# A two-stage attention and channel-mix kernel on one core: deferred gate mixes, another key order, slab weight sums, squares on ScalarE, operand sums on VectorE, another product order

## Chip, core and metric

The kernel runs on one core of a Trainium2 chip. The metric is the device time of one launch in microseconds, here the median of three runs. The engines are named as in the profile: PE is TensorE (PEld is its loading of stationary operands), DVE is VectorE, ACT is ScalarE, POOL is GpSimd, and SP only issues DMAs, in its program order.

## What is computed

The reference is capped attention, whose output x is then mixed and put through a squared-ReLU network with a sigmoid gate. Cut to what matters:

```python
# q, k, v: (8, 12, 448, 64); x: (8, 448, 768)
s = cap * tanh((q @ k.T) / 8 / cap)
a = exp(s - max(s)); a = a / (sum(a) + 1e-9)
x = (a @ v) laid out as (batch, token, 768)
x_prev = x shifted by one token, zero first
xk = mu_k * x + (1 - mu_k) * x_prev
xr = mu_r * x + (1 - mu_r) * x_prev
k = relu(xk @ w_k)            # 768 -> 1024
v = (k * k) @ w_v             # 1024 -> 768
r = sigmoid(xr @ w_r)         # 768 -> 768
out = r * v
```

The three weight matrices come as 64-bit floats and are made into 32-bit floats on the chip. Large products are done as three products of rounded high and low parts (hi·hi, hi·lo, lo·hi).

## The kernel before

**Stage 1.** The 12 heads of a batch are 6 head pairs, so there are 48 pairs, and step i works on several pairs at once. The string `STEP` (L51 to L53) sets the order of operations in a step; each engine executes its own in that order. Scores, tanh, exp and row sums (`red`, L238) belong to pair i; the gather of row sums (`gather`, L243, four DMAs), their reciprocals (`recip`, L247 to L251: sr, rs) and the product with v to pair i-1; `norm` (L263, writes x), the key mix (`mix_old` on ACT, `mix_new` on DVE, tile xk), its high and low parts (POOL, tiles xkh and xkl) and the gate mix to pair i-2. The gate mix is `gate_old` on POOL (L292) and then `gate_new` on DVE (L295), in tile xg, which `x_store` (L299) writes to x_d in DRAM for stage 2. SP issues, in a step: gather (sq<-r), rv<-v, a weight load, rec_store, rqk<-qk, two r<-rec_d, x_d<-xg, and a store of a finished weight; then the next step's gather.

**Keys.** From step 7 on (`LAG`), PE also does the key matmuls of a batch whose six pairs are mixed: 144 of them per batch for 8 columns of blocks (fc), spread over six steps, four calls of six in each. `key_order` (L301) sets their order; a column block needs 18 matmuls (6 dc by 3 parts) into one of two PSUM banks (kps), which ACT empties as ko (L329) and stores to k_d.

**Weights.** 44 pieces of w_k, w_r and w_v are loaded, cleaned on DVE (L381 to L389) and summed on POOL (L396); pieces of w_k also go through POOL wkh (L74) and DVE wkl (L409). In steps 6 to 10 two pieces are loaded a step.

**Stage 2.** There are 28 units of 256 tokens: 14 value units (k·k times w_v) and then 14 gate units (xr times w_r, sigmoid, times v). Each is a 2 by 2 block product by the Strassen-Winograd scheme, with 7 products P1 to P7, one in each slot: 12 matmuls of 128x384 in a value unit's slot, 9 in a gate unit's. `ahead(g)` (L583) issues beside slot g the work of later slots: the loads (src, L481, ten slots ahead), squares (L486, eight ahead), the sums of operand blocks on POOL (`sums2`, L501 to L507, four ahead), and the high part on ACT (L521) and low part on DVE (L522) of the operand two slots ahead. `evacuate` (L540) takes products out of four PSUM banks: p1 is copied, u2 and u3 add it (L556), and the outputs add u2 or u3 (L560).

**Between them.** In the tail (steps 49 to 54) SP loads w_v from DRAM in 16 DMAs of one 128x384 block (L430, L435), and `w2_prep` makes the sums and the high and low parts of seven products' weights, block by block, on DVE (L446 to L466) and ACT (L445); the same is done for w_r during the value units, on DVE and ACT. The code of the prep and the sums is in two places of the program, of which one (for large caps) is not executed.

```python
            for _ in prep:
                pass
            self.k_store()
            self.w2_pool("r", pool("w2r", 1))
            self.w2_loads("r")
            for g in range(2 * NU * SLOTS + 3):
                self.slot(g)
```

Of the kernel before, what the change touches and what calls it, by code (L numbers as in the profile page):

```python
# [1 line left out]

# [7 lines left out]
F32 = mybir.dt.float32  # L10
# [33 lines left out]
P1, P2, P3, P4, P5, P6, P7 = range(7)  # L44

# [6 lines left out]
weight_sum tanh1 exp1 red1 norm recip rec_store K qk_high qk_low tanh2 mix_old mix_new x_high x_low gate_old relu k_store  # L52
K exp2 red2 weight_rest weight_sum relu k_store S3 K K tanh3 exp3 red3 gate_new relu k_store weight_abs load_qk rec_load x_store weight_store"""  # L53
# [6 lines left out]
class Body:  # L60
# [239 lines left out]

    def key_order(self):  # L301
# [120 lines left out]
    def w2_pool(self, kind, pool):  # L422
        n = (NF if kind == "v" else ND) // 2
        self.W2[kind] = tuple(pool.tile([P, 7, n, HN], F32R, name=f"w{kind}{x}") for x in "hl")

    def w2_load(self, kind, j):
        lo = self.W2[kind][1]
        n, at = lo.shape[2], (ND if kind == "v" else 0)
        for m, c, h in ((P1, j, 0), (P3, j + n, 1), (P2, j + n, 0)):
            self.nc.sync.dma_start(f(lo[:, m, j, :]), self.w_d[at + c, :, h * HN:(h + 1) * HN])  # L430

    def b12_load(self, kind, j):
        if j < self.W2[kind][1].shape[2]:
            t = self.b12[kind, j] = self.st.tile([P, HN], F32, name=("p1", "u2")[j % 2])
            self.nc.sync.dma_start(t, self.w_d[j + (ND if kind == "v" else 0), :, HN:])  # L435

    def w2_loads(self, kind):
        for j in range(self.W2[kind][1].shape[2]):
            self.w2_load(kind, j)
            if j < 2:  # L440
                self.b12_load(kind, j)

    def w2_split(self, kind, m, j, x):
        hi, lo = (w[:, m, j, :] for w in self.W2[kind])
# [353 lines left out]
```

## Time and profile before

| what | us |
|---|---|
| median of 3 runs | 1000.93 (1000.39 to 1002.9) |
| the profiled execution, its own time | 998.11 |
| its span, first to last instruction | 995.8 |
| PE busy in the span | 914.0 |
| DVE busy | 801.2 |
| ACT busy | 600.7 |
| POOL busy | 500.8 |

The span is the part of the profiled execution that the trace shows; 2.3 us lie around it. The mean clock granted to TensorE over the span is 0.969 of full speed. The median of the runs is 2.8 us above the profiled execution, so a time worked out on the trace is read on the trace's own scale first.

### The profile page before, as it was taken

To read this page: it belongs to the slowest core of one execution; us is meant where nothing else is said; L and a number is where in the kernel's file an instruction comes from. 1 tells how busy PE (TensorE), PEld (TensorE's weight loads), DVE (VectorE), ACT (ScalarE), POOL (GpSimd) and SP (SyncE) were. 2 spreads that over 40 slices of the span, in tenths; PEclk is the share of its full clock that TensorE was granted. 3 is DMA by queue.
4 is the path that set the end of the run, shared out by engine and by line. 5 is a ranking of instruction groups with operands and counts; after the bars stand their busy time and mean duration, and the time that the engine had idled before them with its cause. 6 is when DMAs were issued, how large, how long until landed. Compare 5 with 4: busy or idle time off the path is not lost.

```text
span 995.8 us, 15130 instructions
## 1 busy us (share of the span) xinstructions
PE 914.0 (92%) x4986; PEld 722.7 (73%) x4986; DVE 801.2 (80%) x1305; ACT 600.7 (60%) x887; POOL 500.8 (50%) x418
## 2 busy tenths in 40 slices
PE   7778779999999999999999777999999999999997
PEld 3235556667666766766676667989898999999996
DVE  7888999888888888887677575898888766887785
ACT  7766657787888887887877333334333334444543
POOL 4667766667666665776653222334342433333331
PEclk9788998999999999999999897999999999999999
DMA  5445544665665566565443535343433326666663
GB/s 157 142 137 166 192 140 163 200 202 186 214 215 175 205 205 206 184 194 185 146 138 99 198 119 175 98 140 97 134 107 117 123 92 203 204 194 208 204 207 115
DMA packets 118871, 163.95 MB, mean 165 GB/s; under 512 B 22400, under 2 KB 102912, under 8 KB 118784
## 3 DMA queue, kind: packets, MB, share of 16 engines
q1 hardware_dynamic: 109568, 148.21, 46.6%
q10 hardware_dynamic: 9216, 14.68, 3.9%
q8 instruction: 41, 0.67, 0.3%
q14 instruction: 46, 0.38, 0.1%
HBM read 106.70 MB, written 53.39 MB: 161 GB/s over the span
## 4 chain that ended last, share of the span: by engine, by line
PE 37%; DVE 22%; POOL 10%; DMA 10%; issue 9%; SPq 5%; ACT 5%; ACTq 0%; DVEq 0%; POOLq 0%
PE ps L537 25%; PE kps L322 6%; DMA sq<-r 4%; SPq L243 4%; PE s L194 3%; DVE r L238 3%; DVE lo L522 3%; POOL xg L292 3%; PE pv L221 3%; DMA src<-x_d 3%; POOL xkl L84 2%; DVE xg L295 2%; ACT p L212 2%; POOL qkl L84 2%; DVE o L560 1%
## 5 line engine op out<-in xcount | busy, mean ns | idle before, releaser
L238 DVE TRANSPOSE_TENSOR_REDUCE r<-p 128x28 f32<-128x896 f32 (+1 forms) x240 | 218.6, 919 | 48.1 <-ACT p L212 43.5
L202 ACT ACTIVATE p<-s,scl_t 128x896 f32<-128x896 f32 x192 | 173.6, 904 | 45.7 <-PE s L194 39.4
L212 ACT ACTIVATE p<-p,cap_t 128x896 f32<-128x896 f32 x192 | 182.0, 948 | 10.2 <-ACT ko L329 5.4
L322 PE MATMUL kps<-xkh,wkh 128*128 128x448 f32 x384 | 147.0, 383 | 16.2 <-ACT ko L329 15.3
L501 POOL TENSOR_TENSOR s<-src 128x512 f32<-128x512 f32 (+1 forms) x28 | 32.6, 1166 | 251.9 <-DVE src L486 154.9
L537 PE MATMUL ps<-wvh,hi 128*128 128x384 f32 x392 | 135.3, 345 | 22.2 <-DVE o L560 11.1
L322 PE MATMUL kps<-xkl,wkh 128*128 128x448 f32 x384 | 140.7, 366 | 0.6 <-POOL xkl L84 0.6
L322 PE MATMUL kps<-xkh,wkl 128*128 128x448 f32 x384 | 140.9, 367 | 0.0
L521 ACT CAST hi<-s 128x512 fp32r<-128x512 f32 (+1 forms) x112 | 63.5, 567 | 118.9 <-PE ps L537 87.0
L537 PE MATMUL ps<-wvl,hi 128*128 128x384 f32 x392 | 132.8, 339 | 0.0
L221 PE MATMUL pv<-p,rv 128*64 128x448 f32 x576 | 132.0, 598 | 0.0
L522 DVE TENSOR_TENSOR lo<-s,hi 128x512 fp32r<-128x512 f32 (+1 forms) x112 | 82.5, 737 | 48.9 <-ACT hi L521 32.1
L194 PE MATMUL s<-qkh 64*128 64x448 f32 (+1 forms) x336 | 85.1, 447 | 29.8 <-ACT p L202 24.9
L396 POOL TENSOR_TENSOR wsq<-wa,wsq 128x384 f32<-128x384 f32 x44 | 44.6, 1014 | 133.9 <-DVE wsq L389 133.9
L521 ACT CAST hi<-src 128x512 fp32r<-128x512 f32 (+1 forms) x84 | 47.7, 568 | 100.3 <-PE ps L537 83.3
L84 POOL TENSOR_TENSOR qkl<-rqk,qkh 128x960 fp32r<-128x960 f32 x47 | 106.2, 2259 | 3.9
L537 PE MATMUL ps<-wrh,hi 128*128 128x384 f32 x294 | 99.9, 340 | 6.2 <-DVE o L560 5.8
L194 PEld LDWEIGHTS s<-qkh 64*128 64x128 f32 (+1 forms) x336 | 37.3, 190 | 86.9 <-ACT p L202 34.9
L322 PEld LDWEIGHTS kps<-xkh,wkh 128*128 128x128 f32 x384 | 72.9, 190 | 37.8 <-ACT ko L329 18.5
L537 PE MATMUL ps<-wrl,hi 128*128 128x384 f32 x294 | 98.7, 336 | 0.0
L522 DVE TENSOR_TENSOR lo<-src,hi 128x512 fp32r<-128x512 f32 (+1 forms) x84 | 74.1, 882 | 28.4 <-PE ps L537 15.1
L537 PEld LDWEIGHTS ps<-wvh,hi 128*128 128x128 f32 x392 | 75.0, 191 | 28.3 <-ACT hi L521 14.7
(93 smaller groups left out, 1854.7 us busy)
## 6 DMA issues: line engine op xcount, KB each, us to landing
rqk<-qk SPq DMA_DIRECT2D x47, 480.0 KB
k_d<-ko ACTq DMA_DIRECT2D x64, 224.0 KB
src<-k_d SPq DMA_DIRECT2D x56, 256.0 KB
rv<-v SPq DMA_DIRECT2D x48, 256.0 KB
r<-rec_d SPq DMA_DIRECT2D x96, 112.0 KB
x_d<-xg SPq DMA_DIRECT2D x48, 224.0 KB
v_d<-o SPq DMA_DIRECT2D x56, 192.0 KB
src<-x_d SPq DMA_DIRECT2D x42, 256.0 KB
```

Source lines behind the costliest of these rows:

```text
L84: {"p": self.nc.gpsimd, "v": self.nc.vector}[e].tensor_sub(*a)
L194: nc.tensor.matmul(s[:, h, 0:S], qk[a][p, k], qk[b][p, 0:S], start=(n == 0), stop=(n == 2))
L202: self.nc.scalar.activation(p32, self.S.pop((i, g))[:, :n, 0:S], AF.Tanh, scale=self.scl_t)
L212: self.nc.scalar.activation(p32, p32, AF.Exp, scale=1.0 if self.maxima else self.cap_t)
L221: nc.tensor.matmul(pv[p, 0:S], v[:, g, h, :], ph[:, h, :], start=(g == 0), stop=False)
L238: self.nc.vector.tensor_reduce(out=out, in_=p32[p, h].rearrange("p h (b k) -> p (h b) k", k=32), axis=mybir.AxisListType.X, op=ALU.add, ap ...
L243: self.nc.sync.dma_start(self.sq[i % 2][:, q], self.r1[i % 2][32 * q:32 * q + 32])
L322: nc.tensor.matmul(self.kps[fc][:, 0:S], w, m[:, dc, :], start=first, stop=last)
L396: {"p": self.nc.gpsimd, "v": self.nc.vector}[e].tensor_add(sq, f(a), sq)
L521: self.nc.scalar.copy(hi, x)
L522: self.nc.vector.tensor_sub(lo, x, f(hi))
L537: self.nc.tensor.matmul(o, a[:, c, :], w[:, c, :], start=first and k == 0, stop=last and k == len(todo) - 1, skip_group_check=True)
```

## The change

It has six parts.

**Gate mixes of pairs 0 to 11.** In steps 2 to 13 `gate_old` and `gate_new` are left out, and `x_store` writes the unmixed x to a new DRAM tensor, raw_d. In steps 36 to 47 `late_load` reads one of them back into xo, and in steps 37 to 48 `late_old` (POOL, behind gate_old) and `late_new` (DVE, behind gate_new) mix it and `late_store` writes it to x_d. On SP late_store and late_load stand between x_store and the next step's gather.

**Key order.** Column block fc1 is taken only 9 matmuls far before fc0 is finished, so that fc0 ends with the 27th matmul and fc1 with the 36th; before, they ended with the 33rd and the 36th. The last three matmuls of fc0 need the sixth pair of the batch; they now begin at the 25th matmul instead of the 31st.

**Weight sums by slabs.** The four blocks of w_v come in four DMAs of 128x4x384 (w_r: 128x3x384) instead of 16 of one block (w_r: 12). The sums and splits act on slabs of 768 columns (w_v, two halves of 11 operations each on DVE or as pairs of ACT and DVE) or 1152 columns (w_r, 11 operations, one a unit). Of w_v's 22 items six are issued in each of steps 50 to 53, none in step 49. The pools around wait for the tiles that they overlap, not for whole pools; the operands of the first unit are issued three slots a step in steps 50 to 53, where it was two a step from step 49.

**Squares** go from DVE to ACT (56 of 128x512). **Operand sums** of the value units go from POOL to DVE (56 of 128x512), and their places become 4 slots before the unit, 2 before, its slot 0 and its slot 1; those of gate units stay on POOL, at the new places.

**Product order** is P1, P6, P5, P7, P2, P4, P3 where it was P1, P6, P2, P7, P5, P4, P3, in all units but the last. The output that takes P5 and P7 can leave its bank one slot earlier, and P3 uses that bank. The loads of v for the gate (`v_load`) come one slot before the unit instead of two.

The core of the diff:

```diff
-weight_sum tanh1 ... x_low gate_old relu k_store
-K exp2 ... gate_new relu k_store weight_abs load_qk rec_load x_store weight_store"""
+weight_sum tanh1 ... x_low gate_old late_old relu k_store
+K exp2 ... gate_new late_new relu k_store weight_abs load_qk rec_load x_store late_store late_load weight_store"""
...
     def x_store(self, i):
-        self.nc.sync.dma_start(self.x_d[i % NP, :, i // NP * S:(i // NP + 1) * S], self.xg)
+        if i >= LATE:
+            self.nc.sync.dma_start(self.x_place(i), self.xg)
+        else:
+            self.nc.sync.dma_start(self.raw_d[i], self.X[i % 2][:, 1:])
+    def late_load(self, i):
+        if i < LATE:
+            self.nc.sync.dma_start(self.xo[:, 1:], self.raw_d[i])
+    def late_old(self, i):
+        if i < LATE:
+            self.xl = self.up.tile([P, S], F32, name="xl", bufs=1)
+            self.nc.gpsimd.tensor_scalar(self.xl, self.xo[:, 0:S], self.om["r"][:, i % NP:i % NP + 1], None, op0=ALU.mult)
+    def late_new(self, i):
+        if i < LATE:
+            self.mix_gate(self.xo, self.xl, i % NP)
+    def late_store(self, i):
+        if i < LATE:
+            self.nc.sync.dma_start(self.x_place(i), self.xl)
...
-        return t[:e] + t[n:n + e] + t[e:n] + t[n + e:2 * n] + t[2 * n:]
+        a = 4 * self.KS - e
+        return t[:e] + t[n:n + a] + t[e:n] + t[n + a:]
...
+        for m, c, h in ((P1, 0, 0), (P7, 0, 1), (P3, n, 1), (P2, n, 0)):
+            self.nc.sync.dma_start(f(lo[m]), self.w_d[at + c:at + c + n, :, h * HN:(h + 1) * HN].rearrange("c p n -> p c n"))
...
+        for m, x, sub in ((P5, a, (a, b12, b11)), (P1, None, ()), (P6, b, (b, b22, a)), (P5, a, ()), (P4, a, (a, b21, b)),
+                          (P6, b, ()), (P7, b, (b, b22, b12)), (P7, b, ()), (P2, None, ()), (P4, a, ()), (P3, None, ())):
+            if sub:
+                self.nc.vector.tensor_sub(*sub)
+            else:
+                self.w2_split(kind, m, k, x)
             yield
...
-        self.nc.vector.tensor_mul(x, x, x)
+        self.nc.scalar.activation(x, x, AF.Square)
...
-        pool = self.nc.gpsimd
+        pool = self.nc.vector if u < NU else self.nc.gpsimd
...
-        return (P1, P6, P2, P7, P5, P4, P3) if u < 2 * NU - 1 else (P1, P6, P5, P7, P4, P3, P2)
+        return (P1, P6, P5, P7, P2, P4, P3) if u < 2 * NU - 1 else (P1, P6, P5, P7, P4, P3, P2)
```

Three places in the order of instructions follow. The first is DVE in one early step, from the key mix to the next row sums, before:

```order
L278 SCALAR_TENSOR_TENSOR xk<-x_157,mu_k,pv 128x448
L238 TENSOR_REDUCE r_0_189<-p_2_607 128x28
L238 TENSOR_REDUCE r_0_189<-p_1_622 64x14 x2
L295 SCALAR_TENSOR_TENSOR xg<-x_157,mu_r,xg 128x448
L409 TENSOR_TENSOR wkl<-wsq,wkh 128x3x128
L381 TENSOR_SCALAR wt<-wsq 128x384
```

The same place on DVE after the change:

```order
L283 SCALAR_TENSOR_TENSOR xk<-x_158,mu_k,pv 128x448
L243 TENSOR_REDUCE r_0_192<-p_2_604 128x28
L243 TENSOR_REDUCE r_0_192<-p_1_617 64x14 x2
L441 TENSOR_TENSOR wkl<-wsq,wkh 128x3x128
L413 TENSOR_SCALAR wt<-wsq 128x384
```

The gate mix xg is gone between the row sums and the weight work behind it.

The second place is SP in a late step, from one gather (sq) to the next, before:

```order
L243 DMA sq_193<-r_0_189 32x112 x4
L151 DMA rv<-v 128x512
L254 DMA rec_d_104<-rs 28x32
L147 DMA rqk<-qk 128x960
L259 DMA r<-rec_d_104 64x448 x2
L299 DMA x_d<-xg 128x448
L243 DMA sq_200<-r_1_196 32x112 x4
```

SP in a late step after the change:

```order
L248 DMA sq_203<-r_1_199 32x112 x4
L156 DMA rv<-v 128x512
L259 DMA rec_d_105<-rs 28x32
L152 DMA rqk<-qk 128x960
L264 DMA r<-rec_d_105 64x448 x2
L312 DMA x_d<-xg 128x448
L331 DMA x_d<-xl 128x448
L318 DMA xo<-raw_d 128x448
L248 DMA sq_196<-r_0_192 32x112 x4
```

Two more DMAs, the store of the late mix (xl) and the load of the next one (xo), stand ahead of the gather.

The third place is SP at the end of stage 1 and the start of stage 2. The tiles wvl and wrl take the weights that are loaded, p and u are scratch, flag is the choice between the program's two copies. Before:

```order
L299 DMA x_d<-xg 128x448
L435 DMA p_6001<-w_d 128x384
L435 DMA u_6053<-w_d 128x384
L481 DMA src<-k_d 128x2x256 x7
L726 TENSOR_LOAD flag
L726 ISA x2
L430 DMA wrl<-w_d 128x384 x3
L435 DMA p_6286<-w_d 128x384
L430 DMA wrl<-w_d 128x384 x3
L435 DMA u_6291<-w_d 128x384
L430 DMA wrl<-w_d 128x384 x3
L481 DMA src<-k_d 128x2x256 x2
```

SP at the same place after the change:

```order
L465 DMA wvl_5952<-w_d 128x4x384
L312 DMA x_d<-xg 128x448
L491 DMA src<-k_d 128x2x256 x7
L743 TENSOR_LOAD flag
L743 ISA x2
L465 DMA wrl_6255<-w_d 128x3x384
L465 DMA wrl_6256<-w_d 128x3x384
L465 DMA wrl_6257<-w_d 128x3x384
L465 DMA wrl_6258<-w_d 128x3x384
L491 DMA src<-k_d 128x2x256 x3
```

Four large wrl loads stand where eleven small ones stood, in both between the seventh src load and the eighth, which is the last of unit 1.

## Rows read from the trace of the kernel before

**Rows 1.** The page, its first part: busy time of each engine over the span, its share, and its instructions.

```profile
PE 914.0 (92%) x4986; PEld 722.7 (73%) x4986; DVE 801.2 (80%) x1305; ACT 600.7 (60%) x887; POOL 500.8 (50%) x418
```

**Rows 2.** Busy time of each engine in stretches of the span: steps 2 to 6, steps 7 to 11, the steady steps before the late ones, the late steps, the tail and the prep of w_v, the value units, the gate units. The columns are the stretch, its length, PE, PEld, DVE, ACT and POOL with their counts, the granted clock of TensorE, the DMA share, GB/s.

```profile
29.50:87.20 57.70, 41.49 (x189) 18.59 (x186) 48.87 (x86) 41.08 (x51) 38.83 (x36) 0.79 0.48 151
87.20:160.10 72.90, 61.75 (x315) 39.92 (x314) 68.66 (x116) 45.44 (x60) 50.36 (x45) 0.91 0.48 157
181.50:433.00 251.50, 247.12 (x1399) 169.74 (x1398) 215.87 (x369) 205.02 (x262) 169.59 (x140) 1.00 0.61 201
433.00:551.40 118.40, 117.66 (x664) 80.75 (x663) 84.60 (x131) 89.55 (x112) 65.68 (x52) 1.00 0.46 146
551.40:600.80 49.40, 34.11 (x155) 29.90 (x153) 33.19 (x56) 18.87 (x40) 12.23 (x10) 0.88 0.48 162
600.80:826.70 225.90, 212.62 (x1177) 206.89 (x1178) 180.54 (x255) 82.34 (x150) 80.26 (x56) 0.98 0.39 124
826.70:989.00 162.30, 156.09 (x882) 152.02 (x882) 126.71 (x221) 78.59 (x166) 55.60 (x52) 1.00 0.60 190
```

**Rows 3.** The timeline of DVE in an early step, from norm (x) to the next norm. The columns are start, duration, engine, line, operation, tiles, and in brackets the idle time ahead and what ended it.

```profile
41.08 0.59 DVE L263 TENSOR_TENSOR x<-pv,r 128x448 f32<-128x448 f32 x1
...
43.34 2.52 DVE L238 TRANSPOSE_TENSOR_REDUCE r<-p 128x28 f32<-128x896 f32 x3
47.28 0.69 DVE L295 SCALAR_TENSOR_TENSOR xg<-x,mu_r,xg 128x448 f32<-128x448 f32 x1 [1.42 <-POOL xg L292]
...
52.62 0.59 DVE L263 TENSOR_TENSOR x<-pv,r 128x448 f32<-128x448 f32 x1
```

**Rows 4.** The timeline of DVE in one of the steps 7 to 11, from norm to the next norm.

```profile
116.28 0.59 DVE L263 TENSOR_TENSOR x<-pv,r 128x448 f32<-128x448 f32 x1
...
119.52 1.11 DVE L238 TRANSPOSE_TENSOR_REDUCE r<-p 128x28 f32<-128x896 f32 x1 [0.99 <-ACT p L212]
...
124.90 0.64 DVE L295 SCALAR_TENSOR_TENSOR xg<-x,mu_r,xg 128x448 f32<-128x448 f32 x1
...
131.16 0.59 DVE L263 TENSOR_TENSOR x<-pv,r 128x448 f32<-128x448 f32 x1
```

**Rows 5.** One late step in three timelines, of DVE, of POOL and of the SP queue: from the reciprocal (sr) over the gate mix and its store to the gather (sq) and the next sr.

```profile
466.62 0.61 DVE L247 TENSOR_REDUCE sr<-sq 32x28 f32<-32x448 f32 x1 [0.71 <-DMA sq<-r]
...
471.71 0.69 DVE L295 SCALAR_TENSOR_TENSOR xg<-x,mu_r,xg 128x448 f32<-128x448 f32 x1 [1.02 <-POOL xg L292]
...
477.74 0.61 DVE L247 TENSOR_REDUCE sr<-sq 32x28 f32<-32x448 f32 x1 [0.75 <-DMA sq<-r]
...
470.27 1.41 POOL L292 TENSOR_SCALAR xg<-x,om_r 128x448 f32<-128x448 f32 x1
...
462.88 2.44 SPq L243 DMA_DIRECT2D sq<-r  x4
...
472.42 0.33 SPq L299 DMA_DIRECT2D x_d<-xg  x1
472.80 2.44 SPq L243 DMA_DIRECT2D sq<-r  x4
```

**Rows 6.** The view of waits over the span: who waited for whom, us in total, how many times, and the longest.

```profile
PE kps L322 <- ACT ko L329: 15.3, 7, 5.2
```

**Rows 7.** The tail and the prep of w_v, in timelines of SP, DVE and PE, and the windows row of a stretch in which the weights' loads fill the queues.

```profile
557.72 1.29 SPq L430 DMA_DIRECT2D wvl<-w_d  x3
...
605.84 0.43 SPq L481 DMA_DIRECT2D src<-k_d  x1
...
563.64 0.55 DVE L455 TENSOR_TENSOR u<-p,wvl 128x384 f32<-128x384 f32 x1
...
567.77 0.74 PE L322 MATMUL kps<-xkh,wkh 128*128 128x448 f32 x1 [5.01 <-ACT ko L329]
...
600.87 0.69 PE L537 MATMUL ps<-wvh,hi 128*128 128x384 f32 x1 [8.94 <-ACT hi L521]
...
564.00:570.00 6.00, 2.23 (x6) 2.01 (x7) 5.16 (x11) 4.16 (x9) 0.00 (x0) 0.58 0.96 336
```

**Rows 8.** The value units. First the windows row of one unit; then groups of instructions by shape from 600 us on (count, busy us, mean ns, idle time just before them and what ended it); last two rows of DVE's timeline while POOL's sums run.

```profile
779.70:794.80 15.10, 14.92 (x84) 14.45 (x84) 10.96 (x17) 5.21 (x9) 5.87 (x4) 1.00 0.39 123
...
L537 PE MATMUL ps<-wvh,hi 128*128 128x384 f32 x392 | 135.3, 345 | 22.2 <-DVE o L560 11.1 <-ACT hi L521 8.9 <-DVE u L556 2.1
...
L522 DVE TENSOR_TENSOR lo<-src,hi 128x512 fp32r<-128x512 f32 x42 | 43.1, 1025 | 15.3 <-PE ps L537 15.1 <-issue 0.2
...
L486 DVE TENSOR_TENSOR src<-src 128x512 f32<-128x512 f32 x52 | 35.6, 684 | 1.8 <-DMA src<-k_d 1.8
...
L521 ACT CAST hi<-src 128x512 fp32r<-128x512 f32 x42 | 26.1, 621 | 63.7 <-PE ps L537 46.9 <-DVE src L486 13.1 <-DVE o L560 3.7
...
727.49 1.64 DVE L446 TENSOR_TENSOR wrl<-wrl,wrh 128x384 fp32r<-128x384 f32 x1
...
730.25 0.54 DVE L556 TENSOR_TENSOR u<-ps,p 128x384 f32<-128x384 f32 x1
```

**Rows 9.** The gate units: a group of PE's matmuls with the idle time ahead of it, and rows of DVE's timeline with and without a sum of POOL beside them.

```profile
L537 PE MATMUL ps<-wrh,hi 128*128 128x384 f32 x294 | 99.9, 340 | 6.2 <-DVE o L560 5.8 <-ACT hi L521 0.4
...
853.32 0.56 DVE L522 TENSOR_TENSOR lo<-s,hi 128x384 fp32r<-128x384 f32 x1 [0.51 <-ACT hi L521]
...
858.10 1.18 DVE L522 TENSOR_TENSOR lo<-src,hi 128x384 fp32r<-128x384 f32 x1
```

More of the change, by code (lines that the diff above doesn't have):

```diff
@@ L1 @@
 from contextlib import ExitStack
+from itertools import chain
 import numpy as np
@@ L120, in init_x @@
             self.X.append(x)
+        self.xo = pool.tile([P, S + 1], F32, name="xo", bufs=1)
+        self.nc.vector.memset(self.xo[:, 0:1], 0.0)
     def init_sums(self, pool):
@@ L423, in w2_pool @@
         n = (NF if kind == "v" else ND) // 2
[L424 to L435, printed above, removed]
@@ L437, in w2_loads @@
-    def w2_loads(self, kind):
[L438 to L444, printed above, removed]
+        self.W2[kind] = lo, hi = {}, {}
+        for x, w in (("l", lo), ("h", hi)):
+            for m in (P1, P7, P3, P2, P5, P6, P4):
+                w[m] = pool[x].tile([P, n, HN], F32R, name=f"w{kind}{x}{m}")
+    def w2_loads(self, kind):
+        lo = self.W2[kind][0]
+        n, at = lo[P1].shape[1], (ND if kind == "v" else 0)
+        for m, c, h in ((P1, 0, 0), (P7, 0, 1), (P3, n, 1), (P2, n, 0)):
+            self.nc.sync.dma_start(f(lo[m]), self.w_d[at + c:at + c + n, :, h * HN:(h + 1) * HN].rearrange("c p n -> p c n"))
@@ L527, in multiply @@
         hi, lo = self.ops.pop((u, i))
-        wh, wl = (w[:, m] for w in self.W2["v" if u < NU else "r"])
+        wl, wh = (w[m] for w in self.W2["v" if u < NU else "r"])
         bank = {P1: 0, P2: 0, P6: 1, P7: 1, P5: 2, P3: 2, P4: 3}[m]
@@ L587, in unit @@
             return (u, s) if 0 <= u < 2 * NU else (None, s)
+        for lag, s, i in ((4, 0, 1), (2, 0, 2), (0, 0, 3), (0, 1, 4)):
+            u, at = unit(lag)
+            if u is not None and at == s:
+                self.sums2(u, i)
         u, s = unit(AHEAD)
@@ L590, in ahead @@
             self.operand(u, s)
-        u, s = unit(4)
-        if u is not None and s < 4:
-            self.sums2(u, s + 1)
         u, s = unit(10)
@@ L599, in ahead @@
             self.square(u, s)
-        u, s = unit(2)
-        if u is not None and u >= NU and s in (0, 2, 3, 4):
-            self.v_load(u, {0: 0, 2: 3, 3: 2, 4: 1}[s])
+        u, s = unit(1)
+        if u is not None and u >= NU and s < 4:
+            self.v_load(u, (3, 0, 2, 1)[s])
     def slot(self, g):
@@ L624, in step @@
         pair.update(dict.fromkeys("norm mix_old mix_new x_high x_low gate_old gate_new x_store".split(), i - 2))
+        pair.update(dict.fromkeys("late_old late_new late_store".split(), i - AT), late_load=i + 1 - AT)
         for op in STEP.split():
@@ L648, in run @@
         KS = NF * ND * 3 // NP // 4
+        self.KS = KS
         self.done, self.ko, self.kps, self.XK = [], [], {}, {}
@@ L714, in run @@
                     sst.close()
-                    self.opp = pool("opp", AHEAD + 1, **right)
+                    self.opp = pool("opp", AHEAD + 1, **tiles)
                     self.ps_2 = pool("ps2", 6, space=PSUM, **right)
-                if i >= tail:
-                    for _ in range(5):
+                else:
+                    for _ in range(6 if i > tail else 0):
                         next(prep, None)
-                    for g in range(first + 2 * (i - tail), first + 2 * (i - tail) + 2):
+                if i > tail:
+                    for g in range(first, min(first + 3, 0)):
                         self.ahead(g)
-            for _ in prep:
-                pass
+                    first += 3
+            assert first >= 0 and next(prep, None) is None
             self.k_store()
```

83 lines of the change are left out of this document (38 added, 45 removed).

## Prediction

> **What bounds the kernel now.** I first read the page's busy shares: PE 92%, DVE 80% [rows 1]. The average hides stages, so next came the windows by stage [rows 2]. In steps 2 to 6 PE is busy 41.5 of 57.7 us and DVE 48.9, in steps 7 to 11 DVE 68.7 of 72.9: there DVE and its exchange with POOL set the pace. From there to 551 us PE is busy over 98% and the clock is full: nothing that leaves DVE, ACT or POOL there helps. The tail and the prep of w_v leave PE idle 15.3 of 49.4 us, the value units 13.3 of 225.9, the gate units 6.2 of 162.3. So the change can win in the first 160 us, in the tail, and in stage 2's gaps; in the late steps, where it puts the deferred mixes, it can only lose.
>
> **Early steps.** Steps 2 to 6: norm to norm is 52.62 - 41.08 = 11.54 us, and DVE's only idle time in it is 1.42 us for POOL's part of the gate mix, followed by 0.69 of its own [rows 3]. Both go: DVE's floor becomes 11.54 - 2.11 = 9.43. What is late next is ACT, 41.08 us in the stretch of five steps [rows 2], 8.2 a step, and the weights' exchange between DVE and POOL. I take 9.8, so 5 x 1.7 = -8.6; between -5 (the 0.69 and a little idle) and -10.5 (all of it). The raw store on SP replaces another store of the same size, and waits only for norm.
>
> Steps 7 to 11: norm to norm is 131.16 - 116.28 = 14.88; DVE's idle time there is 0.99 for tanh and exp on ACT and little else, and xg costs 0.64 [rows 4]. What goes is 0.64 and some waiting and port sharing with POOL: 0.9 a step, -4.5 for five (-2 to -7.5). Steps 12 and 13 are PE's, nothing.
>
> **Key banks.** PE waits seven times in all for ACT to empty a key bank, 15.3 us [rows 6], of which 5.0 stand in the tail [rows 7] and are counted there, and some 5 more in the first batch. The two banks are now finished nine matmuls apart rather than three, so later waits should go. In return the sixth pair's parts are needed at the 25th matmul, the first of a step instead of the middle of one; they are made in the step before. I take -2.5 (0 to -5); where it costs, it is the same few tenths a batch.
>
> **Late steps.** Here is the only loss that I see. The reciprocal sr waits for the gather's DMAs, and SP issues the gather behind the store of xg, which waits for DVE, which waits for POOL, which waits for xk behind the sr before: a loop. From sr to the gather is 472.80 - 466.62 = 6.18, and from the gather to sr 466.62 - 462.88 = 3.74 in one step and 477.74 - 472.80 = 4.94 in the next [rows 5]. The loop takes 9.92 to 11.12 us. The pace is 118.40 / 11 = 10.76 a step [rows 2], set by PE, so there is less than 1 us of slack. The change lengthens the loop: late_old is a second POOL operation of 1.41 ahead of the store (late_new overlaps the rest of it, since late_old doesn't wait for DVE), and the late store and late load are two more issues of 472.80 - 472.42 = 0.38 each, of which the gather sees one more behind late_new and one that xg's store already covers: 1.41 + 0.38 = 1.79. The new loop is 11.71 at the least, 12.91 at the most. I take 11.95, near the short end, since the average of the stretch is itself below the long one. Against 10.76 that is 1.19 a step, 11 steps: **+13**. From below, buffers of p32 and of the two x tiles let PE run ahead by part of a step: +4. From above, the long gather in half of the steps: +20. Behind the gather on SP are rv, rqk and the r loads, and whoever waits for them is in the same loop. POOL is busy 65.7 of 118.4 us there and can take 1.41 a step; DVE too.
>
> **Tail and prep of w_v.** Before, PE loses 5.01 us to a key bank whose relu is queued on ACT behind casts that wait for DVE's prep, and 8.94 at the first product [rows 7]: its keys end at 600.87 - 8.94 = 591.9. The prep is 44 DVE operations of 384 columns, 0.55 each, and starts at 563.64. After: 22 of 768 columns. A subtraction of 384 columns takes 0.55 [rows 7], a square of 512 takes 0.684 [rows 8]; the slope gives 0.96 for 768, so 21.2 us in place of 24.2. SP reaches the loads 0.8 us later; two slabs of 786 KB must land ahead of the first sum, at 336 GB/s [rows 7] 4.7 us, and some 2.5 of latency: about 566, and the prep ends about 587. No prep is issued in step 49, and later relus stand between longer but fewer casts, so the 5.01 should go and the keys end near 587. The value units begin at about 588: **-13**. At the least one of the two waits goes (-6); at most both, and the slow-clock matmuls behind them (-16).
>
> **Value units.** One unit is 84 matmuls in 14.92 us [rows 8]; 14 of them 208.9, where the stage takes 225.9 [rows 2]. Of the 17.0 above, 11.1 are waits of PE for DVE's output add (L560) ahead of P3, whose bank that add must empty [rows 8]. It is late because DVE is slowed: with a sum of POOL's running, a 384-column subtraction takes 1.64 us where 0.55 is its time, and the low parts of 512 columns take 1025 ns in the mean. An operation that reads PSUM is not slowed (0.54) [rows 8]. The change takes POOL's sums away (DVE gets four of about 0.69 a unit, and loses four squares of 0.684: even), and the new product order gives P3 a slot of 2.13 us (14.92 / 7) more. A mean wait of 0.8 doesn't survive that: -11. ACT gains four squares of some 0.62 (its cast of the same shape, 621 ns [rows 8]) a unit, 2.5 us on an engine that is busy 82 of 226. Against it stands the start: the eighth src load is issued behind the loads of w_r (at 605.84, 13.9 us after the keys ended [rows 7]); behind four slabs of 590 KB, 7.0 us at the rate above, it lands about 603, and ACT, which now squares it, holds the fifth and sixth operands behind it: a stall of about 5 us once, and 3 of clock and remainders. 208.9 + 8 = 217: **-9**, between -3 (half the waits stay) and -17.
>
> **Gate units.** 14 units, 156.1 us of PE in 162.3; 5.8 us of waits for the output add ahead of P3 [rows 9]. The later slot takes them away; POOL's sums stay, at new places. I take -2, between -6 and +3.
>
> The Trainium skill ("SBUF — State Buffer", section "Who interferes with whom") has that a DVE instruction with two SBUF inputs and a GpSimd instruction that reads SBUF lock each other out for a whole instruction, while one SBUF input is free of it. The trace agrees: 1.18 against 0.56 for the same low part in the gate units [rows 9]. By that rule the moved sums of the gate units could hold a low part that PE wants: the third rival.
>
> **Sum.** -8.6 - 4.5 - 2.5 + 13 - 13 - 9 - 2 = -26.6. The profiled execution took 998.1, so 971.5 on its scale; the median of the runs lies 2.8 above it, so **974**.
>
> **Rivals.**
>
> 1. The late loop doesn't decide: the buffers between the loop and PE take the 13 us up, or SP gets through sooner. For it: PE is the bound there, and waits on the gather are below 0.8 in the step shown. Against: 11 steps in a row, with less than one of slack. It gives 974 - 11 = 963. Chance 0.13.
>
> 2. The prep isn't earlier: six items a step on DVE and the slabs' landing (nothing can start until 1.57 MB are there, where one block of 0.2 MB was enough) keep the value units from starting before 600. The change then doesn't do what it says in the tail: 974 + 13 = 987. Chance 0.10.
>
> 3. POOL's sums in the gate units hold a low part at each unit: 13 x 0.6 (1.18 - 0.56) = +8 in place of -2, so 984. Chance 0.05.
>
> 4. Slower than before: the squares on ACT. A src load is issued two slots, 4.3 us, ahead of its square; ACT is in order, and an unfinished load blocks the high parts behind it, on which PE waits. With one slot of 2.13 lost in every value unit: 14 x 2.13 = 30, so 1004. It decides from loads that take more than 4.3 us to land as a rule. Against: the same squares on DVE waited for a load 1.8 us in all, in 52 [rows 8]. Chance 0.05.
>
> **How the numbers follow.** The forecast, 974, has 0.67. The range reaches to the tight ends of the terms: the late loop at +4 to +20 and the tail at -6 to -16 move it by 9 up and 12 down, and rivals 1 to 3 end at 963 to 987; with their own spread 955 to 991. A measurement of this kernel tells 0.3%, 3 us, from no change. Faster by more than that: all but rival 4 and a mishap in several terms at once, 0.91; within: 0.03; slower: 0.06.
>
> **What would show it.** Right: norm to norm near 9.8 in steps 2 to 6; sr to sr near 11.9 from 433 us of the old scale on, with PE waiting; the first product about 4 us after the last key matmul at most, and no wait of 5 us for a key bank in the tail; no wait for the output add ahead of P3 in value units; low parts of 512 columns at 0.69 there; one wait for src on ACT in unit 0. Wrong: early steps that stay above 11 us, late steps at 10.8, a first product 9 us after the keys, and waits of PE for high parts in every value unit.

## The result and the profile after

The changed kernel takes 979.0 us (978.2 to 979.4) where the kernel before takes 1000.7 (both are medians of four runs): a ratio of 0.9778, 95% interval 0.9761 to 0.9795. The forecast was 974, range 955 to 991. The profiled execution took 978.96 us, its span is 977.2, where 998.11 and 995.8 stood before.

The first part of the page after the change, to be held against [rows 1]:

```profile
PE 907.9 (93%) x4986; PEld 719.7 (74%) x4986; DVE 757.6 (78%) x1262; ACT 624.0 (64%) x915; POOL 416.8 (43%) x362
```

PE's share has hardly moved, 92% to 93%, although 44 us of DVE's work and 84 of POOL's are gone. What happened is seen by stages again. The windows after the change, with columns as in [rows 2]; the stages are cut at the norms of pairs 0, 5, 10, 13, 35 and 47 and at the first matmuls of the value and gate units (pairs 10 to 13 are left out):

```profile
28.48:76.82 48.34, 38.22 (x191) 17.62 (x188) 45.88 (x81) 40.75 (x51) 31.96 (x31) 0.86 0.58 179
76.82:144.94 68.12, 59.13 (x312) 38.73 (x311) 62.89 (x111) 45.60 (x60) 41.17 (x40) 0.95 0.52 168
176.82:417.43 240.61, 239.41 (x1346) 162.73 (x1345) 205.43 (x353) 194.12 (x250) 161.91 (x134) 1.00 0.63 201
417.43:562.84 145.41, 129.61 (x691) 87.24 (x689) 100.68 (x149) 89.65 (x113) 85.38 (x67) 0.98 0.49 159
562.84:593.63 30.79, 26.43 (x120) 23.42 (x120) 21.67 (x27) 17.09 (x26) 3.09 (x3) 0.94 0.58 203
593.63:807.84 214.21, 207.87 (x1176) 206.52 (x1177) 149.81 (x236) 107.95 (x189) 4.32 (x4) 0.98 0.42 136
807.84:969.28 161.44, 155.80 (x882) 152.06 (x882) 120.50 (x221) 79.94 (x166) 56.18 (x52) 1.00 0.61 193
```

Cut at the same norms and matmuls, the two traces compare so (a stage's length is the difference of two starts in the timelines):

| stage | before | after | difference | forecast |
|---|---|---|---|---|
| start to the norm of pair 0 | 29.55 | 28.48 | -1.1 | 0 |
| steps 2 to 6 | 57.68 | 48.35 | -9.3 | -8.6 |
| steps 7 to 11 | 72.91 | 68.12 | -4.8 | -4.5 |
| steps 12 to 36 | 272.89 | 272.49 | -0.4 | -2.5 |
| late steps, to the norm of pair 47 | 124.70 | 145.40 | +20.7 | +13 |
| tail, to the first product | 43.15 | 30.79 | -12.4 | -13 |
| value units | 225.83 | 214.21 | -11.6 | -9 |
| gate units | 162.31 | 161.44 | -0.9 | -2 |
| end | 6.80 | 7.88 | +1.1 | 0 |
| sum | 995.8 | 977.2 | -18.6 | -26.6 |

The timeline of DVE in an early step, to be held against [rows 3]. The xg and the idle time ahead of it are gone, DVE has no gap, and norm to norm is 57.47 - 47.90 = 9.57 us, where it was 11.54:

```profile
47.90 0.59 DVE L268 TENSOR_TENSOR x<-pv,r 128x448 f32<-128x448 f32 x1
...
50.16 2.53 DVE L243 TRANSPOSE_TENSOR_REDUCE r<-p 128x28 f32<-128x896 f32 x3
52.72 0.56 DVE L441 TENSOR_TENSOR wkl<-wsq,wkh 128x384 fp32r<-128x384 f32 x1
...
57.47 0.59 DVE L268 TENSOR_TENSOR x<-pv,r 128x448 f32<-128x448 f32 x1
```

One late step, in the timelines of DVE, POOL and SP, as in [rows 5]:

```profile
469.83 0.61 DVE L252 TENSOR_REDUCE sr<-sq 32x28 f32<-32x448 f32 x1 [2.06 <-DMA sq<-r]
...
474.89 1.06 DVE L295 SCALAR_TENSOR_TENSOR xg<-x,mu_r,xg 128x448 f32<-128x448 f32 x1 [0.98 <-POOL xg L301]
476.28 1.41 DVE L295 SCALAR_TENSOR_TENSOR xl<-xo,mu_r,xl 128x448 f32<-128x448 f32 x1 [0.33 <-POOL xl L323]
...
482.32 0.61 DVE L252 TENSOR_REDUCE sr<-sq 32x28 f32<-32x448 f32 x1 [2.11 <-DMA sq<-r]
...
474.83 1.41 POOL L323 TENSOR_SCALAR xl<-xo,om_r 128x448 f32<-128x448 f32 x1
...
475.98 0.33 SPq L312 DMA_DIRECT2D x_d<-xg  x1
477.71 0.33 SPq L331 DMA_DIRECT2D x_d<-xl  x1
478.14 0.37 SPq L318 DMA_DIRECT2D xo<-raw_d  x1
478.56 2.45 SPq L248 DMA_DIRECT2D sq<-r  x4
```

DVE waits 2 us for the gather in this step and the next, where it waited 0.7. From sr to the gather is 478.56 - 469.83 = 8.73 us, where it was 6.18, and from the gather to sr 482.32 - 478.56 = 3.76: the loop is 12.49 us and sets the pace. Two of its operations are longer than before: xg takes 1.06 us with POOL's xl running beside it, xl 1.41 with POOL's next work, where such a mix took 0.69 [rows 5]. Only xl's length is on the loop's way: POOL's xl ends at 476.24, 0.29 us after DVE's xg.

The tail, in timelines of SP, DVE and PE, to be held against [rows 7]: the slabs' loads are issued at 563.38 and the first sum starts 6.84 us later; PE's longest wait is for the last pair's key parts on POOL, none for a key bank; the first product follows the keys by 1.06 us of waiting instead of 8.94.

```profile
563.38 2.30 SPq L465 DMA_DIRECT2D wvl<-w_d  x4
...
570.22 0.96 DVE L480 TENSOR_TENSOR src<-wvl,wvl 128x768 f32<-128x768 f32 x1 [1.40 <-DMA wvl<-w_d]
...
565.55 0.47 PE L354 MATMUL kps<-xkh,wkh 128*128 128x448 f32 x1 [3.77 <-POOL xkh L77]
...
593.63 0.44 PE L547 MATMUL ps<-wvh,hi 128*128 128x384 f32 x1 [1.06 <-ACT hi L531]
```

Stage 2 in groups of instructions by shape, as in [rows 8] and [rows 9] (count, busy us, mean ns, idle time ahead and what ended it):

```profile
L547 PE MATMUL ps<-wvh,hi 128*128 128x384 f32 x392 | 132.8, 339 | 7.0 <-ACT hi L531 5.6 <-DVE u L566 1.4
L547 PE MATMUL ps<-wrh,hi 128*128 128x384 f32 x294 | 99.8, 340 | 5.6 <-DVE u L566 5.3 <-DVE o L570 0.3
...
L496 ACT ACTIVATE src<-src 128x512 f32<-128x512 f32 x52 | 32.6, 627 | 8.4 <-DMA src<-k_d 8.4
...
L532 DVE TENSOR_TENSOR lo<-src,hi 128x384 fp32r<-128x384 f32 x42 | 31.9, 759 | 7.9 <-ACT hi L531 7.2 <-DMA src<-x_d 0.3 <-issue 0.3
L532 DVE TENSOR_TENSOR lo<-src,hi 128x512 fp32r<-128x512 f32 x42 | 29.4, 701 | 22.8 <-ACT hi L531 18.4 <-PE ps L547 4.3
```

In the value units the waits for the output add, 11.1 us, are gone, and low parts take 701 ns in place of 1025. What is left, 5.6 us of waits for ACT's high parts, is ahead of and in the first unit: 1.1 ahead of the first product, 1.5, and 3.0 behind a square that waits 7.6 us for its load. Between the first matmuls of successive units lie 24.9 us for the first and 14.56 for each that follows but the last; before, they were 20.9 for the first and 15.1 to 16.7. So the first unit has lost 4.0 us and the other thirteen have won 15.6. In the gate units 5.8 us of waits for the output add have become 5.3 us of waits for u ahead of P7: the wait has moved by some slots and kept its size.

### The profile page after: what moved, and what is told of

Same layout as the page of the kernel before. It is cut to its first block, busy times and chain, and to the rows that moved or that the text cites. A ratio compares the mean times of both kernels' runs of the same rounds, so it can differ in the third digit from the quotient of the medians.

```text
span 977.2 us, 15124 instructions
## 1 busy us (share of the span) xinstructions
PE 907.9 (93%) x4986; PEld 719.7 (74%) x4986; DVE 757.6 (78%) x1262; ACT 624.0 (64%) x915; POOL 416.8 (43%) x362
## 5 line engine op out<-in xcount | busy, mean ns | idle before, releaser
L243 DVE TRANSPOSE_TENSOR_REDUCE r<-p 128x28 f32<-128x896 f32 (+1 forms) x240 | 216.0, 914 | 26.6 <-ACT p L217 22.6
L207 ACT ACTIVATE p<-s,scl_t 128x896 f32<-128x896 f32 x192 | 173.2, 902 | 21.2 <-PE s L199 13.8
L547 PE MATMUL ps<-wvh,hi 128*128 128x384 f32 x392 | 132.8, 339 | 7.0 <-ACT hi L531 5.6
L226 PE MATMUL pv<-p,rv 128*64 128x448 f32 x576 | 128.0, 582 | 5.1 <-DVE xk L283 4.6
L511 POOL TENSOR_TENSOR s<-src 128x384 f32<-128x384 f32 x14 | 14.3, 1025 | 275.3 <-DVE lo L532 271.3
L532 DVE TENSOR_TENSOR lo<-s,hi 128x512 fp32r<-128x512 f32 (+1 forms) x112 | 71.1, 635 | 63.4 <-ACT hi L531 53.5
L199 PE MATMUL s<-qkh 64*128 64x448 f32 (+1 forms) x336 | 84.8, 447 | 29.0 <-ACT p L207 24.2
L354 PEld LDWEIGHTS kps<-xkh,wkh 128*128 128x128 f32 x384 | 73.0, 190 | 34.8 <-issue 12.9
L226 PEld LDWEIGHTS pv<-p,rv 128*64 128x64 f32 x576 | 39.6, 144 | 71.0 <-issue 60.8
L278 ACT ACTIVATE pv<-x,om_k 128x448 f32<-128x448 f32 x48 | 30.6, 638 | 93.8 <-DVE x L268 93.8
```

The lines of the kernel that those rows point to most:

```text
L199: nc.tensor.matmul(s[:, h, 0:S], qk[a][p, k], qk[b][p, 0:S], start=(n == 0), stop=(n == 2))
L207: self.nc.scalar.activation(p32, self.S.pop((i, g))[:, :n, 0:S], AF.Tanh, scale=self.scl_t)
L226: nc.tensor.matmul(pv[p, 0:S], v[:, g, h, :], ph[:, h, :], start=(g == 0), stop=False)
L243: self.nc.vector.tensor_reduce(out=out, in_=p32[p, h].rearrange("p h (b k) -> p (h b) k", k=32), axis=mybir.AxisListType.X, op=ALU.add, ap ...
L278: self.nc.scalar.mul(self.xold, self.X[i % 2][:, 0:S], self.om["k"][:, hp:hp + 1])
L354: nc.tensor.matmul(self.kps[fc][:, 0:S], w, m[:, dc, :], start=first, stop=last)
```

## The experiments

All start from the changed kernel, which is 979.0 us with a ratio of 0.978.

**e1: the late store and load behind the gather.**

```diff
-... rec_load x_store late_store late_load weight_store"""
+gather late_store late_load load_v ...
+... rec_load x_store weight_store"""
...
-        pair.update(dict.fromkeys("late_old late_new late_store".split(), i - AT), late_load=i + 1 - AT)
+        pair.update(dict.fromkeys("late_load late_old late_new".split(), i - AT), late_store=i - 1 - AT)
```

Behind the gather of the next step, the store is that of the pair before, and the load that of the pair that the step mixes.

> The late store and the late load are issued by SP behind the next step's gather instead of ahead of it; POOL and DVE do the same late work. Theory (the loop from sr over the gate mix and its store to the gather decides the late steps): the loop falls back to its old 9.9 us, the late steps take about 10.6 us in place of 12.1, and the time falls by 15 to 20 us, to 959 to 964. Rival (the late work itself, 1.41 us on POOL and 0.69 on DVE a step, is what costs): it stays above 973.

963.6 us, ratio 0.9632 (0.9612 to 0.9652). The late steps, from the norm of pair 35 to that of pair 47:

```profile
417.76:547.67 129.91, 124.98 (x691) 85.76 (x689) 99.94 (x149) 89.64 (x113) 85.70 (x67) 1.00 0.56 179
```

15.5 of the 20.7 us are gone, with the same work on POOL and DVE. The place in SP's queue is the cause of three quarters of the loss. The other 5.2 us stay: the first two late steps, which also clean weights, take 12.9 and 12.5 us (10.4 and 11.4 before), and the last 10.1 (8.6).

**e2: the late mix early in the step**, its store and load still ahead of the gather.

```diff
-weight_sum tanh1 ... mix_new x_high x_low gate_old late_old relu k_store
+late_old weight_sum tanh1 ... mix_new late_new x_high x_low gate_old relu k_store
```

> The late mix is issued early in the step (on POOL ahead of the key parts, on DVE behind the key mix), so that it is done before the store of xg; the late store and load stay ahead of the gather. Theory: of the 1.79 us that the loop gained only the two DMA issues, 0.76, are left; the late steps take about 10.9 us and the time is 964 to 969. Rival (the work costs wherever it stands): no change, 977 to 981.

983.7 us, 0.9822 (0.9806 to 0.9839): slower than the changed kernel by 4.7, and neither expectation. The late steps take 150.6 us. The timeline of POOL in one of them:

```profile
461.24 1.41 POOL L323 TENSOR_SCALAR xl<-xo,om_r 128x448 f32<-128x448 f32 x1 [4.68 <-DMA xo<-raw_d]
```

POOL's late_old now stands at the head of POOL's step and waits there for xo, which SP loads only late in the step before; the work on the next pair's q and k stands behind it, and xkh behind that. So the edit put the operation at another place of the same loop, with a DMA's landing added. It doesn't separate work from issues, which it was meant to do; the run before does.

**e3: no deferral.**

```diff
-LATE = 12
+LATE = 0
```

> No gate mix is deferred (LATE is 0); all else as in the changed kernel. Theory: the early steps lose their gain (9.3 + 4.8 = 14.1 us slower) and the late ones their loss (20.7 us faster), so the deferral as built costs 6 to 7 us and the time is 971 to 974. Rival (the late steps are slow for another reason, such as the key order): 990 or more.

974.6 us, 0.9746 (0.9717 to 0.9774). Steps 2 to 6, 7 to 11 and the late ones:

```profile
28.18:85.82 57.64, 40.41 (x191) 18.43 (x189) 48.84 (x86) 40.92 (x51) 38.77 (x36) 0.82 0.49 151
85.82:158.85 73.03, 61.04 (x315) 40.21 (x314) 67.83 (x116) 45.52 (x60) 50.28 (x45) 0.91 0.49 156
433.11:558.58 125.47, 123.53 (x688) 85.35 (x687) 86.79 (x137) 89.82 (x113) 68.85 (x55) 1.00 0.46 143
```

The early steps are the kernel before's again (57.7 and 72.9 us), and so are the late ones (124.7). The deferral as built brought 14 us in steps 2 to 11 and 1.8 in steps 12 to 36, and cost 20 in the late ones: without it the change is 4.4 us better by the medians, with intervals that overlap a little.

**e4: the old key order.**

```diff
-        a = 4 * self.KS - e
+        a = e
```

> The old key order in the changed kernel. Theory from the two traces (steps 13 to 35 took 239.9 us before and 240.6 after): the order is worth nothing there, and the time is 977 to 981. Rival (the forecast's term, hidden by something else in the steady steps): 981.5 or more; in the tail a wait for a key bank comes back, up to 5 us.

980.4 us, 0.9785 (0.9767 to 0.9802): no difference from the changed kernel. Steps 15 to 36 and the tail:

```profile
179.09:419.62 240.53, 238.67 (x1345) 163.09 (x1345) 206.29 (x354) 195.99 (x250) 162.28 (x134) 1.00 0.63 201
565.73:596.43 30.70, 25.65 (x116) 22.35 (x114) 21.76 (x27) 17.18 (x26) 3.08 (x3) 0.94 0.59 204
```

240.5 and 30.7 us, against 240.6 and 30.8 with the new order. PE does wait more for key banks, and the steps are no longer for it. The view of waits in steps 12 to 36, first of the kernel before, then of the changed kernel, then with the old order in it (us in total, times, longest):

```profile
PE kps L322 <- ACT ko L329: 4.4, 4, 1.8
...
PE kps L354 <- ACT ko L361: 0.3, 1, 0.3
...
PE kps L354 <- ACT ko L361: 2.1, 4, 0.7
```

Of the tail's wait of 5 us 1.0 came back, and the tail's length didn't change, so it wasn't the key order that made the tail shorter.

**e5: the old product order.**

```diff
-        return (P1, P6, P5, P7, P2, P4, P3) if u < 2 * NU - 1 else ...
+        return (P1, P6, P2, P7, P5, P4, P3) if u < 2 * NU - 1 else ...
```

> The old product order in the changed kernel; the value units' sums stay on DVE. If the waits ahead of P3 came from POOL's sums slowing DVE, they stay away without the new order: the value units take 214 to 217 us (214.2 with the new order) and the time is 978 to 982. If the new order's slot of slack took them away, some 11 us come back: 988 to 992. In the gate units the wait for u ahead of P7 goes and that for the output add ahead of P3 comes, 0.46 each: even.

980.9 us, 0.9791 (0.9763 to 0.9818): no difference. PE's groups in value and gate units:

```profile
L547 PE MATMUL ps<-wvh,hi 128*128 128x384 f32 x392 | 132.0, 337 | 7.1 <-ACT p L564 3.4 <-ACT hi L531 2.4 <-DVE o L570 1.3
L547 PE MATMUL ps<-wrh,hi 128*128 128x384 f32 x294 | 99.9, 340 | 6.1 <-DVE o L570 6.1
```

One wait of 1.3 us for the output add in the value units, not twelve of 11.1 us in all; in the gate units, where POOL's sums still run, all of them are back ahead of P3 in place of u ahead of P7.

**e6: the value units' sums on POOL.**

```diff
-        pool = self.nc.vector if u < NU else self.nc.gpsimd
+        pool = self.nc.gpsimd
```

> The value units' operand sums are back on POOL, at their new places; product order stays new. Low parts and weight sums on DVE take 1.2 to 1.6 us again beside them. If the slack of the new order is enough by itself: 978 to 982, with value units of 214 to 217 us. If the lock of the two engines costs at another place (the add u ahead of P7, as in the gate units, 0.4 to 0.5 a unit; or a low part that PE wants): 984 to 992.

983.2 us, 0.9823 (0.9796 to 0.985), between the two times expected; value units of 216.3 us, 2.1 longer (in six traces of kernels that have the changed kernel's value units they take 212.3 to 214.3). The rest of the 4.2 us stands ahead of them in this trace, 1.2 in the tail. DVE is slowed again, and PE waits only 0.8 us more in the group that had waited for the output add:

```profile
L547 PE MATMUL ps<-wvh,hi 128*128 128x384 f32 x392 | 133.1, 340 | 7.8 <-ACT hi L531 7.2 <-DVE o L570 0.6
...
L532 DVE TENSOR_TENSOR lo<-src,hi 128x512 fp32r<-128x512 f32 x42 | 46.0, 1095 | 38.0 <-PE ps L547 29.5 <-ACT hi L531 8.5
```

**e9: both of these together.**

> Old product order and POOL's sums together in the changed kernel; each alone cost the value units 2 us or nothing. If the two are two remedies for one wait (DVE slowed by POOL, ahead of P3), it comes back only now: value units of 222 to 227 us, time 987 to 993. If the wait of the kernel before had another cause that is gone (the prep of w_r by slabs, squares on ACT): value units of 213 to 218, 978 to 984.

1003.3 us, 1.0028 (1.0014 to 1.0042), more than either expectation. The value units, PE's group in them, and the prep of w_r on DVE, with POOL's sums and, last, without them (the changed kernel):

```profile
595.24:830.65 235.41, 212.10 (x1176) 207.34 (x1177) 153.00 (x183) 107.96 (x189) 91.01 (x57) 0.98 0.39 124
...
L547 PE MATMUL ps<-wvh,hi 128*128 128x384 f32 x392 | 134.3, 343 | 23.2 <-DVE o L570 16.8 <-ACT p L564 4.1 <-ACT hi L531 2.4
...
L480 DVE TENSOR_TENSOR st<-wrl,st 128x1152 f32<-128x1152 f32 x2 | 4.9, 2457 | 0.0
...
L480 DVE TENSOR_TENSOR st<-wrl,st 128x1152 f32<-128x1152 f32 x2 | 2.7, 1350 | 0.0
```

Now the waits for the output add are back, 16.8 us: 3.0 in the first unit and 1.2 in each of the second to the twelfth, and the stage is 21.2 us longer than with the two edits. One alone costs nothing and the other 2.1. Each of the two cures the same wait; only without both does it show. The new prep is part of it: the eleven units with the wait of 1.2 us are those with an operation of w_r's prep, which takes 2.11 to 2.46 us beside a sum of POOL and 1.35 without, and the thirteenth unit, which has none, waits 0.3. The stage is 9.6 us longer than before the change; 7.9 of that stand in the first unit (28.8 us, 20.9 before).

**e7: the gate units' sums on DVE.**

```diff
-        pool = self.nc.vector if u < NU else self.nc.gpsimd
+        pool = self.nc.vector
```

> The gate units' operand sums go to DVE too. PE's waits for u ahead of P7, 0.46 a unit, 5.3 us in all, stand in units in which POOL's sums slow DVE's low parts. If that is their cause, they go: 972 to 975. If DVE, which gets 4 sums of 0.54 a unit, is too full or the add stands in line anyway: 978 to 982.

974.0 us, 0.9726 (0.9705 to 0.9748). The gate units take 153.9 us instead of 161.4:

```profile
L547 PE MATMUL ps<-wrh,hi 128*128 128x384 f32 x294 | 99.1, 337 | 0.7 <-DVE u L566 0.3 <-DVE o L570 0.3
...
L532 DVE TENSOR_TENSOR lo<-src,hi 128x384 fp32r<-128x384 f32 x42 | 23.3, 555 | 2.1 <-ACT hi L531 2.0
```

The waits for u go. In the changed kernel a low part of 1.30 us, beside a sum of POOL that runs from 856.31, stands right ahead of u, and PE waits 0.46 us for that u:

```profile
856.43 1.30 DVE L532 TENSOR_TENSOR lo<-src,hi 128x384 fp32r<-128x384 f32 x1 [0.50 <-ACT hi L531]
857.65 0.55 DVE L566 TENSOR_TENSOR u<-ps,p 128x384 f32<-128x384 f32 x1
```

Without POOL's sums the low parts take 555 ns in the mean in place of 759, although DVE has 56 more operations. Of the 7.5 us, 4.9 are waits, the rest is PE's busy time (155.8 to 153.3).

**e8: the eighth src load ahead of w_r's.**

```diff
-            self.w2_loads("r")
             for g in range(2 * NU * SLOTS + 3):
                 self.slot(g)
+                if g == 0:
+                    self.w2_loads("r")
```

> The eighth src load is issued ahead of the loads of w_r. ACT waits 7.6 us for that load to square it, and PE waits 1.5, 1.4 and 3.0 us in the first unit and the next. If the load stands behind the slabs in the queue, the waits go: value units of 209 to 211 us, time 973 to 976. If it is late for another reason: no change.

975.4 us, 0.9738 (0.9704 to 0.9772). The interval overlaps that of the changed kernel; the gain is read from the stage. ACT's squares wait 0.9 us for loads instead of 8.4, and the value units take 208.2 us instead of 214.2:

```profile
L547 PE MATMUL ps<-wvh,hi 128*128 128x384 f32 x392 | 131.5, 335 | 4.0 <-ACT hi L531 2.6 <-DVE u L566 1.4
...
L496 ACT ACTIVATE src<-src 128x512 f32<-128x512 f32 x54 | 33.8, 627 | 0.9 <-DMA src<-k_d 0.9
```

All 6.0 us stand in the first unit, 18.9 us instead of 24.9, though PE's wait was only 3.0. The windows of a stretch of the changed kernel's first unit, and then of the whole first unit in this run:

```profile
610.60:617.50 6.90, 6.01 (x19) 6.01 (x20) 5.81 (x10) 3.42 (x7) 0.00 (x0) 0.51 0.51 155
...
598.11:616.98 18.87, 15.52 (x85) 14.59 (x86) 12.29 (x20) 9.62 (x18) 0.00 (x0) 1.00 0.77 260
```

In the changed kernel the granted clock is down to half, its lower level of 1.2 GHz, from 610.6 us on, in the last microsecond of PE's wait, and 19 matmuls follow one another at some 0.32 us instead of 0.17. That is 2.7 us more, an estimate from these two paces, and with the wait it makes up nearly all of the 6.0.

**e10: squares on DVE.**

```diff
-        self.nc.scalar.activation(x, x, AF.Square)
+        self.nc.vector.tensor_mul(x, x, x)
```

> The squares are back on DVE. If moving them is worth nothing or a little once POOL's sums are gone (DVE has room): 977 to 981. If they hold DVE's sums and low parts up: value units above 218 us, 983 or more. If ACT's wait for the eighth src load was the price of having them on ACT: a gain of up to 5, 974 to 977.

987.2 us, 0.986 (0.9833 to 0.9888); value units of 220.2 us, 6.0 longer. (The rest of the 8.2 us stands in steps 2 to 6, 50.6 us in this trace, which the edit doesn't touch; other runs show that spread too.) 3.9 of the 6 us stand in the first unit, 28.7 us instead of 24.9. There DVE now waits for the eighth load, and u, on which P7 waits, stands behind it. Those two waits, and the windows row of the first unit:

```profile
613.50 0.69 DVE L496 TENSOR_TENSOR src<-src 128x512 f32<-128x512 f32 x1 [6.79 <-DMA src<-k_d]
...
614.80 0.66 PE L547 MATMUL ps<-wvh,hi 128*128 128x384 f32 x1 [9.42 <-DVE u L566]
...
596.88:625.62 28.74, 17.91 (x84) 16.98 (x85) 15.88 (x27) 6.95 (x13) 0.00 (x0) 0.82 0.53 177
```

The other thirteen units take 191.4 us instead of 189.3, 0.17 more in each but the last, with 2.8 us more on DVE each. So two thirds of what the move is worth come from what stands behind a late load: on ACT it held PE up by 3.0 us, on DVE by 9.4. That the move is worth little where the load is early is not shown: no run has the squares on DVE and the load ahead of w_r's.

**e11: the three edits that gained, together.**

> Three edits together: late store and load behind the gather, the eighth src load ahead of w_r's, the gate units' sums on DVE. Their gains by stages were 15.5, 6.0 and 7.5 us; if they add up, 979 - 29 = 950, between 947 and 954. If one hides another: 955 to 962.

950.2 us (946.7 to 952.6), 0.9495 (0.9457 to 0.9533): the sum of the three. The late steps take 128.9 us, the gate units 153.9, and the value units:

```profile
577.02:785.04 208.02, 204.74 (x1177) 203.81 (x1178) 150.10 (x239) 107.97 (x189) 0.00 (x0) 1.00 0.45 140
```

**e12: the same with 10 deferred pairs.**

```diff
-LATE = 12
+LATE = 10
```

> As the run with three edits together, but with 10 deferred pairs instead of 12. Steps 12 and 13 were PE's and gained 1.2 us at most from the deferral, and the first two late steps, which still clean weights, take 12.5 to 12.9 us where the later ones take 10.8: so 1 to 4 us less than that run, 945 to 951. If the first late step is dear wherever it stands: the same as that run.

949.1 us (948.5 to 950.1), 0.9479 (0.9454 to 0.9503): not to be told from the run with 12. The late steps take 127.6 us instead of 128.9, and pairs 10 and 11 lose as much in steps 12 to 14.

## Why the prediction was right, point by point

**Early steps** (-8.6 and -4.5; measured -9.3 and -4.8). Right in mechanism and size. DVE's gap for POOL and its own xg went, and DVE has no gap in the step shown; run e3 brings both stages back to their old lengths.

**Key banks** (-2.5; measured -0.4 in steps 12 to 36). The waits went as forecast, 4.4 us in these steps before and 0.3 after; the step that failed was to count them as time. In the changed kernel the old order has 2.1 us of them (e4), and steps 15 to 36 are as long as with the new. The 0.4 that was gained isn't the order's: steps 12 to 14 are 1.2 us shorter, of which e3, without the deferral, takes 1.0 back, and the forecast had put the deferral at nothing there; steps 15 to 36 are 0.8 longer. What sets a step to 10.9 us in steps 15 to 36, where PE is busy 239.4 of 240.6 us, wasn't tried.

**Late steps** (+13; measured +20.7). The mechanism was right: e1 takes 15.5 us away by the place of two issues alone. The term was too small by 7.7, for three reasons that the trace separates. The step was taken at 11.95 and is 133.45 / 11 = 12.13, over the norms of pairs 35 to 46: 2.0 us. The pace against which it was held, 10.76, was that of the stretch to 551 us; over the same eleven norms it was 116.06 / 11 = 10.55: 2.3 us. And the step to the norm of pair 47, which the forecast's eleven steps leave out, went from 8.64 to 11.95: 3.3 us; DVE's wait for the gather in it grew from 1.7 to 4.3. The loop itself is 12.49 in the step shown, with the short gather. From sr to the gather it grew by 2.55 us and not by 1.79. The difference is late_new: on the way to the gather it stands in the place of xg, for which the sum had 0.69 us, and it takes 1.41 beside POOL's next operation.

**Tail** (-13; measured -12.4). Right in both waits: that for a key bank is gone, and the first product follows the keys by 1.06 us. That the key order isn't the cause is shown by e4. Which part of the new prep is, the slabs, its later start or the pools that wait for single tiles, was argued and not tried. The prep took 24.2 us, from 570.22 to 594.46, where 21.2 was forecast.

**Value units** (-9; measured -11.6). Right in the waits that went and in the one that came: PE waits 3.0 us behind the eighth load, forecast as about 5, and with the slow stretch behind it e8 takes 6.0 away, where 8 was forecast for the whole start. Two sizes were off and cancelled in part: a unit without waits takes 14.56 us and not 14.92, 5 us less in fourteen, and the first unit lasts 10.3 longer than that and not 8. The prediction gave the 11 us to two causes together. Runs e5, e6 and e9 show that they don't add: either is enough.

**Gate units** (-2; measured -0.9). The step that failed was that the later slot takes the waits away: the wait ahead of P3 became one ahead of P7, so that the new order gained nothing there. The third rival came in part: POOL's sums do hold a low part, but PE doesn't want that part; it wants the u behind it, and waits 0.46 a unit. The cause is shown by e7, which removes it. The Trainium skill ("SBUF — State Buffer", section "Who interferes with whom") has it that a DVE instruction with two SBUF inputs and a GpSimd instruction that reads SBUF shut each other out. The trace agrees: 759 ns for a low part with POOL's sums in the stage, 555 without them. That one SBUF input is free of it, as the prediction has it, the same section of the Trainium skill says only of instructions outside the two-port modes. In the trace before, a DVE tensor_scalar with one SBUF input (wa<-wt, at 91.10) took 1.21 us beside POOL's operations and 0.36 without.

**The other rivals.** The late loop did decide (e1), so the first is out. The first product was earlier, so the second is out. The fourth, a block of ACT at each unit, showed in the first unit and not again: 8.4 us of waiting for loads in 52 squares, 7.6 of them one load's.

In sum: on the profiled executions the change brought 19.2 us where 26.6 were forecast. The late steps account for 7.7 of the difference, the keys for 2.1, the gate units for 1.1; the value units and the early steps gave back 3.6. The medians differ by 21.7 us, since the profiled execution of the kernel before was one of its shorter ones, 2.6 below its median, and that of the changed kernel stands at its median.

That the forecast came within 5.0 us of the measured 979.0 is in part luck. On the trace's own scale it was 971.5 against 978.96, 7.5 off; the 2.8 us that were added for the median were no longer there after the change, and hid a third of the miss. The terms' errors also partly cancel. And the range was worked out wrongly: the ends that are named for the late loop and the tail move the forecast by 14 up and not by 9; 955 to 991 holds that too.

## What to carry to other kernels

Work that is put off to a stage with idle engines isn't free there: look at which in-order queue it passes, and put its DMAs behind those that a loop waits for. Hold a lengthened loop against the pace of the very steps that it will stand in, the last ones too, where the engine that covered it has run out. Before crediting one of two edits that work on the same wait, undo both: two remedies for one wait each look worthless when undone alone.

## What the runs showed of the hardware

An operation of POOL is dear to DVE: DVE's operations with two operands in SBUF went from 1.35 to 2.46 us (1152 columns) and from 0.69 to 1.06 and 1.41 (448 columns) beside one. Taking 56 sums from POOL and giving them to DVE made DVE's low parts faster, 555 ns in place of 759, and the gate units 7.5 us shorter.

A wait of PE of 3.0 us in the first value unit cost 6.0 (e8): TensorE's granted clock fell to half at its end, and the matmuls of the next microseconds followed one another at 0.32 us instead of 0.17. Without the wait the clock of that unit was 1.00.

Steps 2 to 6 took 48.2 to 50.7 us in twelve traces of kernels that do the same work in them. So a difference of 2 us in this stage between two single traces is not a finding, and none is made one here; what sets this spread wasn't tried.
